# A convolution and channel-mix kernel: its start written out in a fixed order, with a first step of 256 tokens, small first groups and a new order of loads

## The chip, the cores and the metric

The kernel runs on one core of one Trainium2 chip. The time is device microseconds (us) of that core. A core has TensorE (PE; PEld is its weight load), VectorE (DVE), ScalarE (ACT), GpSimd (POOL) and SyncE (SP). They run side by side and wait for one another through semaphores. SBUF is the working memory, PSUM the memory that TensorE writes. DMAs are issued here from two queues: SP's and POOL's.

## What is computed

The input `x` is 8 batches x 4160 tokens x 192 channels. A causal convolution over 7 tokens, with softmax weights per head (8 heads of 24 channels), is followed by a channel mix:

```python
# convolution: w = softmax(weight, axis=-1); 8 heads x 7 taps
out = np.einsum('hk,bskhg->bshg', w, x_unf)            # x_unf: the 7 tokens up to s
# channel mix, on x = out
x_prev = np.concatenate([zeros, x[:, :-1, :]], axis=1)
xk = mu_k * x + (1.0 - mu_k) * x_prev
xr = mu_r * x + (1.0 - mu_r) * x_prev
k = np.maximum(xk @ w_k, 0.0)                          # 192 -> 1024
v = k * k @ w_v                                        # 1024 -> 192
r = 1.0 / (1.0 + np.exp(-(xr @ w_r)))                  # 192 -> 192
return r * v
```

## The kernel before

**Tiling.** Batches are worked on in four pairs `p`. Of a pair, both batches go through the same instructions. The convolution works in blocks of 112 tokens (38 blocks cover 4160 tokens), and several blocks make a group: 9 or 10, for the first pair 5, 5, 10, 9 and 9. For a group, POOL loads x as bf16 with the halo of 6 tokens (`load_x`, lines 71-95). `conv_mm` (193-205) multiplies a head's 24 channels of all blocks by a banded (Toeplitz) matrix `toe`, one matmul and one PSUM bank a head. `conv_out` (207-219) copies the result to `y`, whose channels are kept as 128 of batch one, 128 of batch two, and the last 64 of both together. Then tokens and channels are exchanged: for the early groups on TensorE (`tr_mm` 246-258, up to six transposes of two blocks, and `tr_out` 260-268 on DVE), for all others by writing `y` to DRAM and reading it back through a transposing DMA (`y_write` 229-236, `y_read` 238-243, both on SP).

**Channel mix.** Steps have 512 tokens of both batches, the last of a pair 64. `diff` (275-286) and four `mix` (288-321) make `xk` and `xr` on DVE. Each step has eight slots, one for 128 of the 1024 hidden channels: `k_mm` (329-355) on TensorE, `k_relu` (378-384) on ACT, `k_square` (386-396) on DVE. The output side goes in tiles of 128 tokens: `r_mm` and `r_sig` (400-421), `v_mm` with eight matmuls (423-437), `v_out` (439-456) with the store on SP.

**Order.** All engines work through their instructions in the order in which the code gives them. Four tables (`early`, `pe`, `act`, `dve`) hold what is done in which slot `n`, and slots are worked off in pairs (516-530): first the early loads, then the k matmuls of both slots, then for each slot ACT's copies, TensorE's other matmuls, the relu, DVE's work and the square of the slot before. A v tile is worked on ten slots after the k slot of the same number (`LAG_V`). Slots run from -60, so the same tables also give the start: group 0 is convolved from slot -22 on, with ACT and DVE taking turns at its copies, group 1 from slot -7 on, step 0 is mixed from slot -7 to -2. A matmul that needs a PSUM buffer waits for the copy that empties it; the convolution, the transposes and r share two buffers (`psM`), k has two (`psK`) and v two (`psV`).

**The start (lines 98-187).** SP loads the convolution weights and the six pieces of `mu`. 36 matmuls on constants (122-126) keep TensorE busy; they read `ones_t` and the zeroed `w_row`. DVE and ACT compute the softmax into `w_row` (127-144), SP writes it to DRAM (`w_scr`) and reads it back, shifted per partition, as `toe` (146-155). POOL loads x of group 0 at once; then a copy from `w_row` (186) holds its queue until the softmax is there; then follow `wk`, x of group 1, `wr`, `wv` and further x. POOL's DMAs take turns at eight semaphores, so a DMA waits until the one eight places before it has landed. The three buffers of `xb` also hold loads back until an older group is convolved.

Lines of helpers that appear in the profile: L88 is the large x load, L124 the warm-up, L139 the last step of the softmax, L199 the convolution, L216 and L219 its copies, L254 and L265 transposes and their copies, L281 `diff`, L303 `mix`, L343 and L350 the two halves of k, L382 relu, L396 square, L412 and L413 r, L421 sigmoid, L431 v, L443 output.

Of the kernel before, what the change touches and what calls it, by code (L numbers as in the profile page):

```python
# [7 lines left out]
FP32 = mybir.dt.float32  # L8
# [6 lines left out]
def kernel(  # L15
# [23 lines left out]
    NBLK = -(-S // BLK)  # L39
    STEP = 512  # L40
    NSTEP = S // STEP
    TAIL = S - NSTEP * STEP
    NPAIR = B // 2
    SPP = NSTEP * NF + 1
    NSLOT = NPAIR * SPP
    YC = 16
    LAG_V = NF + 2
    WARM = 36
    LAG_R = NF
# [11 lines left out]
    groups = [  # L61
        [(0, 10, 0), (10, 10, 2), (20, 9, 4), (29, 9, 6)]
        if p
        else [(0, 5, 0), (5, 5, 1), (10, 10, 2), (20, 9, 4), (29, 9, 6)]
        for p in range(NPAIR)
    ]
# [4 lines left out]
    def load_x(p, g):  # L71
        blk0, nb, _ = groups[p][g]
        xb = three.tile([P, GB, 2, D], BF16, tag="xb", name="xb")
        xbs[p, g] = xb
        for s in range(2):
            b = 2 * p + s
            lo, hi = 0, nb
            if blk0 == 0:
                lo = 1
                nc.gpsimd.memset(xb[0:32, 0, s, :], 0.0)  # L80
                nc.gpsimd.dma_start(out=xb[HALO:P, 0, s, :], in_=x[b, 0 : P - HALO, :])
            t0 = blk0 * BLK - HALO
            if blk0 + nb == NBLK:
                hi = nb - 1
                r0 = t0 + hi * BLK
                nc.gpsimd.memset(xb[:, hi, s, :], 0.0)
                nc.gpsimd.dma_start(out=xb[0 : S - r0, hi, s, :], in_=x[b, r0:S, :])
# [11 lines left out]
    nc.sync.dma_start(  # L99
        out=w_raw,  # L100
        in_=bass.AP(tensor=weight.tensor, offset=weight.offset, ap=[[0, P], [K, H], [1, K]]),
    )
    nc.scalar.preload_act_table(AF.Exp)
    ones_t = const.tile([P, P], BF16)
    nc.vector.memset(ones_t, 1.0)
# [3 lines left out]
    nc.vector.memset(w_row, 0.0)  # L109
    load_x(0, 0)  # L110
    ident = const.tile([P, P], BF16)
    nc.gpsimd.affine_select(
        out=ident,
        in_=ones_t,
        pattern=[[1, P]],
        compare_op=ALU.is_equal,
        fill=0.0,
        base=0,
        channel_multiplier=-1,
    )  # L120

    warm = psM.tile([P, 4, P], FP32, tag="m", name="warm")
    for _ in range(WARM):
        nc.tensor.matmul(  # L124
            out=warm, lhsT=ones_t, rhs=w_row[:, 0:4, :], start=True, stop=True
        )
    w_max = const.tile([P, H], FP32)
    nc.vector.tensor_reduce(out=w_max, in_=w_raw, axis=mybir.AxisListType.X, op=ALU.max)
    w_exp = const.tile([P, H, K], FP32)
    nc.vector.tensor_tensor(  # L130
        out=w_exp, in0=w_raw, in1=w_max.unsqueeze(2).to_broadcast([P, H, K]), op=ALU.subtract
    )
    nc.scalar.activation(out=w_exp, in_=w_exp, func=AF.Exp)
    w_sig = const.tile([P, 1], FP32)
    nc.scalar.activation(out=w_sig, in_=w_exp[:, 0, 0:1], func=AF.Sigmoid)
    w_sum = const.tile([P, H], FP32)
    nc.vector.tensor_reduce(out=w_sum, in_=w_exp, axis=mybir.AxisListType.X, op=ALU.add)
    nc.vector.reciprocal(out=w_sum, in_=w_sum)
    nc.vector.tensor_tensor(  # L139
        out=w_row[:, :, 0:K],  # L140
        in0=w_exp[:, :, ::-1],
        in1=w_sum.unsqueeze(2).to_broadcast([P, H, K]),
        op=ALU.mult,
    )
    w_scr = dram.tile([P, H, P], BF16)
    nc.sync.dma_start(out=w_scr, in_=w_row)
    toe = const.tile([P, H, BLK], BF16)
    nc.sync.dma_start(
        out=toe,
        in_=bass.AP(  # L150
            tensor=w_scr.tensor,
            offset=w_scr.offset + K - 1,
            ap=[[H * P - 1, P], [P, H], [1, BLK]],
        ),
    )


    mu = const.tile([P, 2, 2], FP32)
    for i, m in enumerate((moe_mu_k, moe_mu_r)):
        nc.sync.dma_start(out=mu[:, i, 0:1], in_=m[0:P])  # L160
        nc.sync.dma_start(out=mu[0:LO, i, 1:2], in_=m[P:D])
        nc.sync.dma_start(out=mu[LO:P, i, 1:2], in_=m[P:D])
# [8 lines left out]
    def load_w(w, src):  # L171
        nc.gpsimd.dma_start(out=w[:, 0, :], in_=src[0:P, :])
        nc.gpsimd.dma_start(out=w[0:LO, 1, :], in_=src[P:D, :])
        nc.gpsimd.dma_start(out=w[LO:P, 1, :], in_=src[P:D, :])

    def load_rest():
        load_w(wr, moe_w_r)
        nc.gpsimd.memset(wr[:, 2:4, :], 0.0)
        nc.gpsimd.tensor_copy(out=wr[0:LO, 2, :], in_=wr[0:LO, 1, :])
        nc.gpsimd.tensor_copy(out=wr[LO:P, 3, :], in_=wr[LO:P, 1, :])  # L180
        nc.gpsimd.dma_start(out=wv, in_=moe_w_v.rearrange("(f p) d -> p f d", p=P))
        for t in tails:
            nc.gpsimd.memset(t, 0.0)

    gate = const.tile([P, 1], BF16)
    nc.gpsimd.tensor_copy(out=gate, in_=w_row[:, 0, 0:1])
    load_w(wk, moe_w_k)


    ys, yTs = {}, {}  # L190
    conv_ps = {}

    def conv_mm(p, g, h):
        nb = groups[p][g][1]
        if h == 0:
            ys[p, g] = two.tile([P, GB, 2 * D], BF16, tag="y", name="y")
        ps = psM.tile([P, GB, 2, G], FP32, tag="m", name="ps_c")
        conv_ps[p, g, h] = ps
        nc.tensor.matmul(  # L199
            out=ps[:BLK, :nb],  # L200
            lhsT=toe[:, h, :],
            rhs=xbs[p, g][:, :nb, :, h * G : (h + 1) * G],
            start=True,
            stop=True,
        )
# [355 lines left out]
```

## Time and profile before

| | |
|---|---|
| time, median of three runs | 486.33 us (485.29 to 487.19) |
| the profiled execution | 485.83 us, of it span from first to last instruction 484.1 us |
| mean granted TensorE clock | 0.979 |
| busy: PE, DVE, ACT, POOL | 459.3, 390.5, 374.6, 51.9 us |
| PE without any idle time | from 54.6 to 470 us |
| first convolution matmul, first relu | 20.94 us, 31.03 us |

The profile is one execution. Times are from the span's start. A releaser named behind `<-` is what ended an idle time. The granted clock is the share of full speed that TensorE's throttle gave in a stretch.

### The profile page before, as it was taken

The page shows a single profiled execution, that of the slowest core. Times are in us where ns is not written, and L with a number is a line of the kernel's source. Part 1 is how long each engine was busy: PE and PEld are TensorE (multiplying, and loading weights), DVE is VectorE, ACT ScalarE, POOL GpSimd, SP SyncE. Part 2 cuts the span into 40 slices and gives each one's busy share as a digit, 9 for nine tenths or more (in the row PEclk, how much of TensorE's full clock was granted, in tenths as well). Part 3 has the DMA queues.
Part 4 walks back from the last instruction along what each step waited for, and adds up shares of the span by engine and source line. Part 5 has one row for each costly group of instructions (what it writes and reads, how often), then busy time and mean ns, then how long its engine had stood idle before and what let it go on. Part 6 is the DMA issues. An engine that isn't in the chain of part 4 may idle for free.

```text
span 484.1 us, 9846 instructions
## 1 busy us (share of the span) xinstructions
PE 459.3 (95%) x3920; PEld 299.0 (62%) x3920; DVE 390.5 (81%) x607; ACT 374.6 (77%) x544; POOL 51.9 (11%) x84
## 2 busy tenths in 40 slices
PE   8167799999999999999999999999999999999996
PEld 3133466666667666666667666666667666666676
DVE  1165698989889887988889887988889887999873
ACT  2137879798887889798887889798887879777772
POOL 3560401002030101002030101002000000000000
PEclk9668999999999999999999999999999999999999
DMA  3898696938959492948759392947935351712112
GB/s 43 133 154 100 96 188 140 208 110 157 167 125 216 83 249 67 186 132 154 172 119 217 78 233 86 190 134 144 180 121 139 108 144 53 190 67 67 67 57 99
DMA packets 137837, 65.03 MB, mean 134 GB/s; under 512 B 89344, under 2 KB 137408, under 8 KB 137792
## 3 DMA queue, kind: packets, MB, share of 16 engines
q1 hardware_dynamic: 97200, 48.80, 41.8%
q0 software_dynamic: 40592, 15.62, 28.0%
q8 instruction: 30, 0.49, 0.5%
q14 instruction: 15, 0.12, 0.1%
HBM read 31.49 MB, written 37.18 MB: 142 GB/s over the span
## 4 chain that ended last, share of the span: by engine, by line
PE 90%; DMA 4%; ACT 2%; POOL 2%; DVE 1%; issue 0%; DVEq 0%; POOLq 0%
PE ps_v L431 35%; PE ps_k L343 25%; PE ps_k L350 14%; PE ps_c L199 4%; PE ps_r L413 4%; PE ps_r L412 4%; DMA xb<-in_x_dram 3%; PE warm L124 2%; DMA wr<-in_moe_w_r_dram 1%; POOL xb L88 1%; ACT k_sb L382 1%; ACT y L216 1%; ACT y L219 0%; PE ps_t L254 0%; PE ps_k L370 0%; PE ps_k L363 0%
## 5 line engine op out<-in xcount | busy, mean ns | idle before, releaser
L382 ACT ACTIVATE k_sb<-ps_k 128x1024 bf16<-128x1024 f32 x260 | 259.9, 1027 | 34.3 <-PE ps_k L350 30.8
L431 PE MATMUL ps_v<-wv,k 128*128 128x192 bf16 x2048 | 210.8, 246 | 0.0
L431 PEld LDWEIGHTS <-k 128*128 128x128 bf16 x2048 | 175.2, 98 | 30.3
L396 DVE TENSOR_TENSOR k<-k_sb 128x1024 bf16<-128x1024 bf16 x256 | 175.0, 684 | 20.2 <-ACT k_sb L382 19.6
L343 PE MATMUL ps_k<-xk,wk 128*128 128x512 bf16 x512 | 155.2, 385 | 0.0
L443 DVE TENSOR_TENSOR o_sb<-ps_v,r_sb 128x384 f32<-128x384 f32 x132 | 72.3, 547 | 36.7 <-PE ps_v L431 35.4
L421 ACT ACTIVATE r_sb<-ps_r 128x384 bf16<-128x384 f32 x132 | 64.2, 486 | 40.8 <-PE ps_r L413 40.8
L350 PE MATMUL ps_k<-xk,wk 64*128 64x512 bf16 x512 | 78.7, 385 | 0.0
L343 PEld LDWEIGHTS <-wk 128*128 128x128 bf16 x512 | 37.7, 97 | 54.5 <-issue 53.9
L216 ACT CAST y<-ps_c 112x480 bf16<-112x480 f32 (+5 forms) x99 | 47.8, 489 | 23.8 <-PE ps_c L199 19.7
L303 DVE SCALAR_TENSOR_TENSOR xk<-d,mu,yT 128x1024 bf16<-128x1024 bf16 x64 | 64.7, 1013 | 0.1
L303 DVE SCALAR_TENSOR_TENSOR xr<-d,mu,yT 128x1024 bf16<-128x1024 bf16 x64 | 64.5, 1012 | 0.1
L199 PE MATMUL ps_c<-xb,toe 128*112 128x432 bf16 (+2 forms) x136 | 47.6, 359 | 17.3 <-DMA toe<-w_scr 9.1
L412 PE MATMUL ps_r<-wr,xr 128*128 128x192 bf16 x256 | 63.0, 246 | 1.0 <-ACT y L219 1.0
L413 PE MATMUL ps_r<-wr,xr 128*128 128x192 bf16 x256 | 63.0, 246 | 0.0
L350 PEld LDWEIGHTS <-wk 64*128 64x128 bf16 x512 | 15.9, 94 | 56.1 <-issue 55.6
L88 POOL DMA_DIRECT2D xb<-in_x_dram x34 | 32.4, 957 | 119.7 <-PE ps_c L199 69.0
L199 PEld LDWEIGHTS <-toe 128*112 128x112 bf16 x136 | 18.4, 136 | 26.5 <-DMA toe<-w_scr 9.6
L281 DVE TENSOR_TENSOR d<-yT 128x1536 bf16<-128x1536 bf16 (+1 forms) x36 | 31.6, 877 | 0.1
L219 ACT CAST y<-ps_c 112x432 bf16<-112x432 f32 (+5 forms) x49 | 24.7, 511 | 1.7 <-PE ps_c L199 1.6
L413 PEld LDWEIGHTS <-xr 128*128 128x128 bf16 x256 | 25.0, 98 | 1.3 <-issue 1.2
L412 PEld LDWEIGHTS <-xr 128*128 128x128 bf16 x256 | 25.0, 98 | 0.8 <-issue 0.7
(52 smaller groups left out, 91.0 us busy)
## 6 DMA issues: line engine op xcount, KB each, us to landing
out_dram<-o_sb SPq DMA_DIRECT2D x128, 192.0 KB, 2.2
xb<-in_x_dram POOLq DMA_DIRECT2D x14, 432.0 KB, 11.8
y_dram<-y SPq DMA_DIRECT2D x8, 756.0 KB, 7.0
y_dram<-y SPq DMA_DIRECT2D x6, 840.0 KB, 5.5
xb<-in_x_dram POOLq DMA_DIRECT2D x8, 480.0 KB, 11.1
xb<-in_x_dram POOLq DMA_DIRECT2D x8, 384.0 KB, 9.6
xb<-in_x_dram POOLq DMA_DIRECT2D x2, 240.0 KB, 7.1
xb<-in_x_dram POOLq DMA_DIRECT2D x2, 192.0 KB, 4.4
```

Of the source, the lines that this page charges most:

```text
L199: nc.tensor.matmul(out=ps[:BLK, :nb], lhsT=toe[:, h, :], rhs=xbs[p, g][:, :nb, :, h * G : (h + 1) * G], start=True, stop=True,)
L216: copy(out=yh[:, :, :, c0 : c0 + n], in_=ps[:BLK, :nb, :, 0:n])
L303: nc.vector.scalar_tensor_tensor(out=o, in0=d[r0:r1, sl, :L], scalar=mu[r0:r1, i, part : part + 1], in1=yT[r0:r1, sl, c0 : c0 + L], op0=AL ...
L343: nc.tensor.matmul(out=ps[:, i, :], lhsT=wk[:, 0, fs], rhs=xk[:, i, :], start=first, stop=not first)
L350: nc.tensor.matmul(out=ps[:, i, :], lhsT=wk[r, 1, fs], rhs=xk[r, 2, :], start=not first, stop=first)
L382: nc.scalar.activation(out=k_sb, in_=ps.rearrange("p a b -> p (a b)"), func=AF.Relu)
L396: nc.vector.tensor_tensor(out=o, in0=k_sb, in1=k_sb, op=ALU.mult)
L412: nc.tensor.matmul(out=o, lhsT=hi, rhs=wr[:, 0, :], start=True, stop=False)
L413: nc.tensor.matmul(out=o, lhsT=lo, rhs=wlo, start=False, stop=True)
L421: nc.scalar.activation(out=r_sb[:, :n, :], in_=ps[:, :n, :], func=AF.Sigmoid)
L431: nc.tensor.matmul(out=o, lhsT=k2[:, f, t * P : (t + 1) * P], rhs=wv[:, f, :], start=(f == 0), stop=(f == NF - 1),)
L443: nc.vector.tensor_tensor(out=o_sb[:, :n, :], in0=v_ps.pop(m)[:, :n, :], in1=r_sbs.pop(m)[:, :n, :], op=ALU.mult)
```

## The change

The work ahead of the first slot no longer comes out of the slot tables: `prologue()` writes it out in one fixed order, and slots begin at 0. In it:

- The first pair has steps of 256, seven of 512, 256 and 64 tokens instead of eight of 512 and one of 64. A step of 256 has four slots, each with two times 128 hidden channels, so that a slot has the same number of columns.
- The groups of the first pair have 3, 4, 5, 4, 10, 6 and 6 blocks. The first four are transposed on TensorE, the last three through DRAM. Small groups put up to three heads into one PSUM bank (`chunks`), with one copy for all of them; in the prologue the convolution uses `psM` and `psV` in turn.
- The warm-up has 34 matmuls and reads an own tile `zeros`.
- Memsets of the x halo and of `wr` go from POOL to DVE. The two copies inside `wr` become two more loads of the same rows.
- `toe` is read on POOL's queue; behind it follow `wk`, x of group 2, `wr`, `wv`, x of group 3. The copy that held POOL back is gone. SP loads `mu` after writing `w_scr`.
- The slots of the first groups' work are set anew (`late`, `per`).

```diff
-    WARM = 36
+    WARM = 34
...
+    for p in range(NPAIR):
+        sizes = [STEP // 2] + [STEP] * (S // STEP - 1) + [STEP // 2] if p == 0 else [STEP] * (S // STEP)
...
+        for nb, s, on_pe in (
+            ((3, 0, True), (4, 1, True), (5, 2, True), (4, 3, True), (10, 4, False), (6, 6, False), (6, 7, False))
+            if p == 0
+            else ((10, 0, False), (10, 2, False), (9, 4, False), (9, 6, False))
+        ):
...
+    def chunks(g):
+        n = max(1, min(3, BANK // (2 * G * groups[g][2])))
+        return [range(h, min(H, h + n)) for h in range(0, H, n)]
...
+        def go(hi, start):
+            for f in range(nf):
+                fs = slice((j * nf + f) * P, (j * nf + f + 1) * P)
+                for i in range(2):
+                    r = slice(0, P) if hi else slice(i * LO, (i + 1) * LO)
+                    nc.tensor.matmul(
+                        out=ps[:, i, f * L : (f + 1) * L],
...
+            at_ = n0 + ns + 2
+            tiles.append((s, t, max(at_, tiles[-1][2] + 1) if tiles else at_))
...
+        late = p == 0 and n0 < 30
+        if not on_pe:
+            per = 2 if late else 1
+            c0 = n0 - 20 if late else n0 - 30
+            w0, r0 = c0 + -(-nc_ // per), n0 - (11 if late else 17)
+        else:
+            per = 1
+            c0 = n0 - 14 if n0 > 12 else 1
+            r0 = c0 + nc_ + 1
...
+    def prologue():
...
+        nc.vector.memset(ones_t, 1.0)
+        nc.vector.memset(zeros, 0.0)
+        x_tile(0, nc.vector)
+        x_tile(1, nc.vector)
+        x_tile(2, nc.vector)
+        nc.vector.memset(w_row, 0.0)
+        nc.vector.memset(wr[:, 2:4, :], 0.0)
+        load_x(0)
+        load_x(1)
...
+        warm = psK.tile([P, BANK], FP32, tag="k", name="warm")
+        for _ in range(WARM):
+            nc.tensor.matmul(out=warm, lhsT=ones_t, rhs=zeros, start=True, stop=True)
+        softmax()
+        nc.sync.dma_start(out=w_scr, in_=w_row)
+        load_toe()
+        load_wk()
+        load_x(2)
+        load_wr()
+        load_wv()
...
+        for c in range(n):
+            conv_mm(0, c, psV if c % 2 else None, "v" if c % 2 else "m")
+        for c in range(n):
+            conv_out(0, c, act_ if c % 2 == 0 else dve_, act_)
+        for j in range(2):
+            tr_mm(0, j)
+        for j in range(2):
+            tr_out(0, j, dve_)
+        n = len(chunks(1))
+        for c in range(n):
+            conv_mm(1, c, psV if c % 2 else None, "v" if c % 2 else "m")
+            conv_out(1, c, act_)
+        diff(0)
+        for i in range(2):
+            for part in range(2):
+                mix(0, i, part)
+        for j in range(2):
+            tr_mm(1, j)
+            tr_out(1, j, dve_)
+        x_tile(3, nc.vector)
+        load_x(3)
```

Three places show how rows move. On POOL's queue, from the making of the identity matrix on, there stood before (a name in brackets is a semaphore; `DMASW` are those of POOL's own DMAs, `DMAHW` those of SP's):

```order
L112 AFFINE_SELECT ident<-ones_t 128x128 [waits DVE_49]
L186 COPY gate<-w_row 128x1 [waits DVE_49]
L172 DMA wk<-in_moe_w_k_dram 128x1024
L173 DMA wk<-in_moe_w_k_dram 64x1024
L174 DMA wk<-in_moe_w_k_dram 64x1024
L88 DMA xb<-in_x_dram 128x5x192
L88 DMA xb<-in_x_dram 128x5x192 [waits DMASW0_49]
L172 DMA wr<-in_moe_w_r_dram 128x192 [waits DMASW1_49]
```

and there stands now, at the same place:

```order
L527 AFFINE_SELECT ident<-ones_t 128x128
L174 DMA toe<-w_scr 128x8x112 [waits DMAHW1_49]
L142 DMA wk<-in_moe_w_k_dram 128x1024
L143 DMA wk<-in_moe_w_k_dram 64x1024 [waits DMASW0_49]
L144 DMA wk<-in_moe_w_k_dram 64x1024 [waits DMASW1_49]
L109 DMA xb<-in_x_dram 128x5x192 [waits DMASW2_49]
L109 DMA xb<-in_x_dram 128x5x192 [waits DMASW3_49]
L147 DMA wr<-in_moe_w_r_dram 128x192 [waits DMASW4_49]
```

The copy that waited for the softmax is gone, the toe load with its wait for `w_scr` stands ahead of all weights, and the x load in this row is that of group 2, since group 1 went out before.

On DVE, from the last step of the softmax to the first step's mix, there stood before:

```order
L139 TENSOR_TENSOR w_row<-w_exp,w_sum 128x8x7 [waits DVE_49,PE_49]
L216 CAST y<-ps_c 112x5x2x24 [waits PE_49] x2
L216 CAST y<-ps_c 112x5x2x8 [waits PE_49]
L219 CAST y<-ps_c 112x5x2x16
L219 CAST y<-ps_c 112x5x2x24 [waits PE_49]
L226 MEMSET yT 128x3x8
L265 COPY yT<-ps_t 128x3x224 [waits PE_49] x2
L265 COPY yT<-ps_t 128x3x112 [waits PE_49]
L281 TENSOR_TENSOR d<-yT 128x1536 [waits DVE_49]
L303 SCALAR_TENSOR_TENSOR xk<-d,mu,yT 128x1024 [waits DMAHW1_49,DVE_49]
```

and there stands now:

```order
L166 TENSOR_TENSOR w_row<-w_exp,w_sum 128x8x7 [waits DVE_49]
L219 CAST y<-ps_c 112x3x2x56 [waits PE_49]
L227 MEMSET yT 128x3x8
L268 COPY yT<-ps_t 128x3x224 [waits PE_49]
L268 COPY yT<-ps_t 128x3x112 [waits PE_49]
L281 TENSOR_TENSOR d<-yT 128x3x256 [waits DVE_49]
L301 SCALAR_TENSOR_TENSOR xk<-d,mu,yT 128x2x256 [waits DMAHW2_49,DVE_49]
```

The softmax's last step no longer waits for PE, one copy of group 0 is left on DVE, and difference and mix are half as long.

On ACT, from the first relu on, there stood before (copies of groups of 10 and 9 blocks between the relus):

```order
L382 ACTIVATE k_sb<-ps_k 128x1024 [waits PE_49]
L219 CAST y<-ps_c 112x5x2x24 [waits PE_49]
L382 ACTIVATE k_sb<-ps_k 128x1024
L216 CAST y<-ps_c 112x10x2x24 [waits DVE_49,PE_49,Activation_49]
L382 ACTIVATE k_sb<-ps_k 128x1024 [waits PE_49]
L216 CAST y<-ps_c 112x10x2x24 [waits PE_49]
L216 CAST y<-ps_c 112x9x2x24 [waits PE_49,Activation_49]
L382 ACTIVATE k_sb<-ps_k 128x1024
```

and there stands now:

```order
L372 ACTIVATE k_sb<-ps_k 128x1024 [waits PE_49] x2
L219 CAST y<-ps_c 112x5x2x48 [waits PE_49,Activation_49]
L372 ACTIVATE k_sb<-ps_k 128x1024 [waits PE_49]
L219 CAST y<-ps_c 112x5x2x48 [waits PE_49]
L372 ACTIVATE k_sb<-ps_k 128x1024
L219 CAST y<-ps_c 112x5x2x32 [waits PE_49]
L222 CAST y<-ps_c 112x5x2x16
L372 ACTIVATE k_sb<-ps_k 128x1024 [waits DVE_49,PE_49]
```

Between the first relus stand copies of group 2, two heads each; those of the group of ten blocks come from slot 9 on.

More of the change, by code (lines that the diff above doesn't have):

```diff
@@ L108 @@
     w_row = const.tile([P, H, P], BF16)
[L109 to L136, printed above, removed]
@@ L185 @@
[L185 to L190, printed above, removed]
-    conv_ps = {}
[L193 to L205, printed above, removed]
@@ L357, in k_mm_tail @@
-    def k_mm_tail(n):
-        p, s, f = where(n)
+        s, j = slots[n]
+        p, _, L, _, _ = steps[s]
+        if L == TAIL:
+            return k_mm_tail(n, p)
+        xk = xks[s]
+        ps = psK.tile([P, 2, BANK], FP32, tag="k", name="ps_k")
+        k_ps[n] = ps
+        first = j % 2 == 0
+        nf = STEP // L
+        def go(hi, start):
[3 more added lines that the diff above has]
+                    r = slice(0, P) if hi else slice(i * LO, (i + 1) * LO)
+                    nc.tensor.matmul(
+                        out=ps[:, i, f * L : (f + 1) * L],
+                        lhsT=wk[r, 0 if hi else 1, fs],
+                        rhs=xk[r, i if hi else 2, :L],
+                        start=start and f == 0,
+                        stop=not start and f == nf - 1,
+                    )
@@ L518, with bundles @@
+    def bundles():
+        n = 0
+        while n < tiles[-1][2] + 3:
+            w = 2 if n < NSLOT and steps[slots[n][0]][2] > TAIL else 1
+            yield range(n, n + w)
+            n += w
+    with tc.manual_schedule():
+        prologue()
+        for n in range(-60, 0):
+            for table in (early, act, pe, dve):
+                assert n not in table, n
+        for ns in bundles():
             for n in ns:
                 run(early, n)
-            real = [n for n in ns if 0 <= n < NSLOT]
+            real = [n for n in ns if n < NSLOT]
```

433 lines of the change are left out of this document (226 added, 207 removed).

## The prediction

> **What bounds the kernel now.** I read the profile's stages first (busy time of each engine between two moments of the span), because the page's shares mix a start-up with a steady state. Columns: stretch, length, then busy time of PE, PEld, DVE, ACT and POOL with instruction counts, granted clock, DMA share, GB/s.
>
> ```profile
> 0.00:12.00 12.00, 10.17 (x36) 4.08 (x36) 1.62 (x7) 3.02 (x4) 3.71 (x11) 1.00 0.40 43
> 12.00:21.00 9.00, 0.06 (x1) 0.06 (x2) 0.09 (x1) 0.00 (x0) 5.65 (x10) 0.75 1.05 162
> 21.00:30.00 9.00, 7.04 (x32) 4.01 (x32) 5.91 (x13) 3.82 (x12) 6.37 (x9) 0.50 0.88 91
> 30.00:42.00 12.00, 7.85 (x35) 2.81 (x34) 5.07 (x9) 4.66 (x7) 3.42 (x6) 0.71 1.59 190
> 42.00:54.60 12.60, 8.77 (x47) 3.81 (x47) 9.59 (x14) 12.11 (x22) 2.29 (x5) 1.00 0.12 14
> 54.60:470.00 415.40, 415.40 (x3651) 274.39 (x3649) 363.32 (x559) 347.16 (x493) 30.46 (x44) 1.00 0.71 141
> ```
>
> From 54.6 to 470 us TensorE is never idle at full clock: there only TensorE work counts, and the change adds or removes hardly any. All that can be won lies before 54.6: warm-up matmuls on constants, 9 us of nothing, 21 us at half or mixed clock, and 12.6 us in which ACT is the full engine (12.11 of 12.60). The chain that ended last and the list of waits name the causes.
>
> ```profile
> 1.67 10.18 PE warm L124 x36
> 28.12 12.99 DMA xb<-in_x_dram
> ```
>
> ```profile
> DVE w_row L139 <- PE warm L124: 6.0, 1, 6.0
> PE ps_c L199 <- DMA toe<-w_scr: 9.1, 1, 9.1
> PE ps_c L199 <- DMA xb<-in_x_dram: 3.6, 2, 3.0
> ```
>
> The softmax result is kept back 6.0 us by the warm-up (which reads `w_row`), TensorE then waits 9.1 us for `toe`, and later 3.6 us for x of the third and fourth group. The timeline gives the moments:
>
> ```profile
> 5.64 0.20 DVE L138 RECIPROCAL w_sum<-w_sum 128x8 f32<-128x8 f32 x1
> 11.87 0.22 DVE L139 TENSOR_TENSOR w_row<-w_exp,w_sum 128x56 bf16<-128x56 f32 x1 [6.03 <-PE warm L124]
> 20.94 0.65 PE L199 MATMUL ps_c<-xb,toe 128*112 128x240 bf16 x2 [9.11 <-DMA toe<-w_scr]
> 31.03 1.02 ACT L382 ACTIVATE k_sb<-ps_k 128x1024 bf16<-128x1024 f32 x1 [1.04 <-PE ps_k L350]
> ```
>
> **The measure.** Since the end is TensorE without a gap, the time is decided by TensorE's debt when that stretch begins: the moment minus the useful TensorE work done by then, at full-clock prices. The prices are in the chain behind 54.6 (start, length, what):
>
> ```profile
> 54.80 0.43 PE ps_k L343 x2
> 55.23 0.54 PE ps_k L350 x4
> 55.77 0.54 PE ps_k L343 x2
> 56.31 0.30 PE ps_t L254 x6
> 56.61 0.66 PE ps_v L431 x8
> 57.27 0.08 PE ps_r L412
> 70.13 0.18 PE ps_c L199
> ```
>
> The first three rows are two k slots: 1.51, so 0.755 a slot. A v tile is 0.66, an r tile 2 x 0.08 = 0.16, six transposes 0.30 (0.15 a block of 112 tokens), a convolution matmul of nine blocks 0.18 (0.02 a block and head, 0.16 a block). Before, at 54.6, ten slots (7.55), the convolution of 5+5+10+9 = 29 blocks (4.64), transposes of ten blocks and six more (1.8) and one r tile (0.16) are done: 14.2. **Debt before: 54.6 - 14.2 = 40.4 us.**
>
> **The change part by part.** *Softmax and toe.* The warm-up now reads `zeros`, so `w_row` loses its wait for PE and starts where the reciprocal ends: 5.84 + 0.22, about 6.1 instead of 12.1. The memsets that DVE gets now (zeros, x halo, wr) stand ahead of the softmax, where DVE only waits for the weights to land; that wait covers them, and beyond it they would delay `w_row` one for one. The transfers, with KB each and median us from issue to landing; the row under them is the shortest, median and longest landing of the large x loads, and the last is what POOL pays to issue one (mean ns):
>
> ```profile
> w_scr<-w_row SPq DMA_DIRECT2D x1, 256.0 KB, 2.0
> toe<-w_scr SPq DMA_DIRECT2D x1, 224.0 KB, 6.7
> xb<-in_x_dram POOLq DMA_DIRECT2D x2, 192.0 KB, 4.4
> xb<-in_x_dram POOLq DMA_DIRECT2D x2, 240.0 KB, 7.1
> wk<-in_moe_w_k_dram POOLq DMA_DIRECT2D x1, 256.0 KB, 4.8
> y_dram<-y SPq DMA_DIRECT2D x8, 756.0 KB, 7.0
> yT<-y_dram SPq DMA_TRANSPOSE x14, 8.9
> DMA to landing us min/median/max: 4.4/10.1/17.9
> L88 POOL DMA_DIRECT2D xb<-in_x_dram x14 | 13.2, 949 | 0.3 <-issue 0.3
> ```
>
> `w_scr` goes out at 6.1 and lands 2.0 later; with first x loads beside it I take toe's issue at 8.4. On POOL the toe load is ahead of wk, x and wr, and what is queued behind its wait is exactly those. Toe itself: not below 4.4 (192 KB with nothing beside it), not above 6.7 (what it took beside wk and x); I take 5.0, nearer the first, since only the end of two x loads is ahead of it. **Toe at T = 13.4** (12.8 to 15.1) instead of 20.9. The mu loads now follow `w_scr` on SP; they are first read about T + 4, so they have some 7 us.
>
> The page "DMA: Bandwidth & Descriptors" of the Trainium skill (Specifications) gives a first-byte latency of about 1 us on the GpSimd path and 0.6 on the SyncE path, which speaks against moving toe to POOL; by it the sum would be 0.4 us longer, an estimate that no run here shows.
>
> *From toe to the first relu.* Before it took 31.03 - 20.94 = 10.1 us, with five blocks a group, 512 tokens and half clock. The prices on ACT and DVE (busy, mean ns):
>
> ```profile
> L382 ACT ACTIVATE k_sb<-ps_k 128x1024 bf16<-128x1024 f32 x13 | 13.9, 1078 | 2.0 <-PE ps_k L350 2.0
> L216 ACT CAST y<-ps_c 112x480 bf16<-112x480 f32 x5 | 2.9, 578 | 4.4 <-issue 3.2 <-PE ps_c L199 1.3
> L216 ACT CAST y<-ps_c 112x240 bf16<-112x240 f32 x8 | 2.7, 358 | 18.8 <-PE ps_c L199 18.5
> L421 ACT ACTIVATE r_sb<-ps_r 128x384 bf16<-128x384 f32 x2 | 1.0, 492 | 1.1 <-PE ps_r L413 1.1
> L265 DVE COPY yT<-ps_t 128x672 bf16<-128x672 bf16 x7 | 3.5, 507 | 9.6 <-PE ps_t L254 9.5
> L281 DVE TENSOR_TENSOR d<-yT 128x1536 bf16<-128x1536 bf16 x3 | 2.9, 958 | 0.1
> ```
>
> Between the two copy rows a copy of other size is read off a straight line (432 elements 0.53, 384 0.49, 288 0.40). Group 0: matmuls and their latency 0.45, ACT's copies with one wait for DVE 1.55, so T + 2.0; nine transposes 0.5; two DVE copies 0.5 + 0.35, T + 3.4. Only then are its PSUM buffers free for group 1, whose five ACT copies take 2.1: T + 5.6; its transposes stand on PE ahead of the first k matmul: T + 6.6; one slot and its latency 1.0: **first relu at T + 7.6 = 21.0**, 10 us earlier than before. DVE's half-size difference and mixes (0.5 + 0.5 + 0.4 after T + 3.4) hide under group 1, as does wk (issued by 12.3, landing 4.8 later, 17.1). Bounds 7 to 10.1 for the stretch.
>
> *The first fourteen slots.* v tiles of whole steps now begin at slot 14. ACT has to do, slots 0 to 13: 14 relus x 1.08 = 15.1; copies of group 2 (three of 480, and 320 + 160) 2.4; of group 3 (three of 384, and 256 + 128) 2.1; of group 4 (seven of 480, and 320 + 160) 4.8; two sigmoids 1.0. Sum 25.4; before, ACT was busy 12.11 of 12.60 in such a stretch, 96%, so 26.4. The k matmuls of slot 14 start about a relu before relu 14: T + 7.6 + 26.4 - 1.0 = **46.4**. TensorE's work by then: 14 slots 10.6; convolution of 3+4+5+4+10 = 26 blocks 4.2; transposes of 16 blocks 2.4; four v tiles 2.6; six r tiles 1.0: 20.8. **Debt after: 46.4 - 20.8 = 25.6.** The stretch can be 2 us shorter (no bubble, relus at 1.0) or 4 longer, since four matmuls in a row now pass two PSUM buffers.
>
> *Loads behind toe.* At 0.95 an issue: wk to 12.2, x of group 2 to 14.1, landing 7.1 after its issue, 20.3; the x load of group 3 waits for that landing, group 4's two follow, the last issued at 22.2. At the median 10.1 it lands at 32.3. Its first matmul is in slot 8: eight relus, group 2, one copy of group 3 and the sigmoids are 12.5 / 0.96 = 13 us after T + 7.6, less one for TensorE's lead: 33. In time by 0.7 us; cost 0, and 7 if it takes the longest landing, 17.9.
>
> *Steady part and end.* The rest of the order is the same rows, in other group sizes for the first pair; ACT has spare time there (347 of 415). Half-size matmuls are more in number, but columns are equal: 0, at most 0.5. The transposed read of group 4 is asked for in slot 17 and needed by DVE in slot 21; DVE will wait. Write out at 45.4, 7.0, then 8.9: 61.3. TensorE can go on to slot 24's v tile: 46.4 + 10 x 1.70 (0.755 + 0.66 + 0.16 + six blocks 0.12) = 63.4, less the difference, square and output that DVE owes first, 2.2: 61.2. Cover just holds: 0.
>
> **Sum.** The profiled execution took 485.8 (span 484.1, 1.7 around it), 0.5 under the median of the three runs, 486.3. Debt falls by 40.4 - 25.6 = 14.8: 485.8 - 14.8 = **471.0**.
>
> **Rivals.** *A: as summed.* For it: every stretch has its price in a row. 0.52, with 467 to 474 from the bounds above (toe -0.6 to +1.7, first relu to +2.5, ACT -2 to +4, not all at once).
>
> *B: the x stream is late.* For it: before, the longest piece of the chain is an x load (12.99), and the load of group 4 has 0.7 us to spare by the median. Against: fewer bytes are ahead of it, and TensorE waits for x only twice in all (3.6 us). At 17.9 it lands at 40.1, TensorE and ACT stand 7.1 in slot 8: 478; half of it, 474.5. 0.22.
>
> *C: the clock falls in the sparse prologue.* The clock in the third column from the end:
>
> ```profile
> 16.00:18.00 2.00, 0.00 (x0) 0.00 (x0) 0.00 (x0) 0.00 (x0) 1.81 (x4) 0.62 1.11 198
> 32.00:34.00 2.00, 1.32 (x8) 0.61 (x6) 1.07 (x2) 1.33 (x3) 1.06 (x3) 0.62 1.60 191
> ```
>
> A mean of 0.62 over 2 us is a quarter at full and the rest at half: it fell near 16.5, 4.6 us after the last warm-up matmul (1.67 + 10.18 = 11.85), and came back near 33.5, 12.6 us after TensorE resumed. Now the warm-up of 34 ends near 11.3, and toe is 2.1 us behind: not long enough by that row. But from T to T + 6.6 TensorE has about 2.5 us of work, and the clock may fall there. Then for up to 12.6 us a slot costs TensorE some 1.3 x 2 = 2.6 us against ACT's 26.4 / 14 = 1.9: 0.7 over nearly five slots, 3.4, and about 1 in the prologue: 475.4. 0.18. The page "TensorE: Matmul & The Clock Gate" of the Trainium skill (Part 1) has the clock back after one busy window of about 3.4 us; by it this rival would cost about 1 us and 1 in the prologue, 473. The trace speaks against so short a time here: PE was busy 2 of 2 us at half clock between 30 and 32 and 7.04 of 9 before, and the clock stayed down.
>
> *D: the transposed read of group 4 stops DVE.* Its place is the difference in slot 21, asked for four slots earlier instead of ten. With the read landed at 61.2 it costs nothing; each us later costs one, since TensorE then waits for PSUM that DVE must empty. If both the write and the read take as long as the longest x load (17.9), it lands at 45.4 + 35.8 = 81.2: 20 us, 491, slower than before; it decides from 76 on. Against: the medians are 7.0 and 8.9, and the x loads beside it are smaller. 0.03.
>
> *E: less waiting than summed* (toe near 12.8, ACT without bubbles): 464 to 467. 0.05.
>
> **How the numbers follow.** The likeliest is A, 471.0. The range takes A, most of B and C: 465 to 478; outside are D, the low half of E and the worst of B and of several delays together, under 2 in 10. A measurement of this kernel can tell about 0.5% (2.4 us) from no change: 483.9 to 488.7. A, B, C and E are faster than that, 0.97, of which I keep 0.02 for delays that add up to no change: faster 0.95, same 0.02, slower 0.03.
>
> **What would show it.** In the profile after: `w_row` without a wait for PE, near 6; the first convolution near 13.4; the first relu near 21; TensorE without idle time from about 46 on; the wait for x in slot 8 under 1 us; granted clock 1.0 from 12 on (C: 0.5 somewhere in 14 to 30). Wrong would be: toe later than 15, ACT under 90% between 22 and 46, a DVE wait for `yT` that TensorE feels, or a gap-free stretch that begins after 50.

## The result, and the profile after

The changed kernel takes **469.03 us** (468.94 to 469.93, four runs); the kernel before took 486.76 beside it (485.29 to 488.14). The ratio is 0.964, with a 95% interval of 0.961 to 0.967. Forecast: 471.0, within 465 to 478. The profiled execution took 468.94, its span is 467.2 instead of 484.1: 16.9 us less.

The stages after: stretch, length, busy time of PE, PEld, DVE, ACT and POOL with counts, granted clock, DMA share, GB/s.

```profile
0.00:12.00 12.00, 8.94 (x34) 3.67 (x34) 2.39 (x10) 3.02 (x4) 7.07 (x15) 1.00 0.72 92
14.00:21.00 7.00, 5.55 (x41) 3.95 (x41) 5.71 (x12) 2.46 (x9) 6.85 (x12) 0.54 1.36 163
21.00:44.70 23.70, 19.86 (x157) 11.51 (x157) 19.14 (x30) 21.20 (x35) 5.62 (x8) 0.99 1.04 129
46.00:452.00 406.00, 397.81 (x3514) 269.67 (x3572) 356.11 (x554) 341.49 (x494) 29.58 (x36) 1.00 0.70 144
```

The 9 us without work are gone, half clock fills only the prologue, and the first fourteen slots lie from 21 to 45. The 8 us that TensorE lacks in the last row aren't idle time: 3514 matmuls are recorded beside 3572 weight loads. From 46 us to the end the list of TensorE's waits has this one entry:

```profile
PE ps_k L343 <- issue: 0.2, 1, 0.2
```

The chain, first piece by piece to the first convolution, then through DVE ahead of slot 14, and into the gap-free stretch (start, length, what):

```profile
0.80 2.88 DMA w_raw<-in_weight_dram
...
4.96 0.23 DVE w_row L166
...
5.21 4.21 DMA w_scr<-w_row
...
9.71 3.44 DMA toe<-w_scr
...
38.79 0.56 DVE o_sb L446
39.35 0.60 DVE k L391
39.95 1.20 DVE xr L301
41.15 0.60 DVE k L391
41.75 0.43 DVE yT L268
...
42.22 0.36 PE ps_c L199
...
44.72 1.58 PE ps_k L343 x8
...
46.42 0.66 PE ps_v L433 x8
```

`w_row` is ready at 5.2, nine tenths of a microsecond earlier than forecast (the weights land 2.88 after their issue, with no `mu` loads beside them now); `w_scr` takes twice what it took before; toe, with 3.44 instead of 5.0, makes up for it. The v tile of slot 14 starts at 46.42, its k matmuls at 44.72. The timeline beside it:

```profile
13.19 0.71 PE L199 MATMUL ps_c<-xb,toe 128*112 128x144 bf16 x8 [2.86 <-DMA toe<-w_scr]
20.90 2.06 ACT L372 ACTIVATE k_sb<-ps_k 128x1024 bf16<-128x1024 f32 x2 [2.61 <-PE ps_k L343]
46.26 0.82 PE L433 MATMUL ps_v<-wv,k 128*128 128x192 bf16 x8
```

First convolution 13.19 (forecast 13.4), first relu 20.90 (21.0). The timeline merges the v tile with a convolution matmul ahead of it, hence 46.26; this row is what the runs below are compared by. TensorE has no wait for x in its list, and DVE waits 0.2 us for the transposed read:

```profile
PE ps_c L199 <- DMA toe<-w_scr: 2.9, 1, 2.9
DVE d L281 <- DMA yT<-y_dram: 0.2, 1, 0.2
```

### The profile page after: what moved, and what is told of

It is laid out like the page before. It is cut to its first block, busy times and chain, and to the rows that moved or that the text cites. A ratio compares the mean times of both kernels' runs of the same rounds, so it can differ in the third digit from the quotient of the medians.

```text
span 467.2 us, 9868 instructions
## 1 busy us (share of the span) xinstructions
PE 445.2 (95%) x3892; PEld 300.6 (64%) x3954; DVE 390.4 (84%) x616; ACT 374.6 (80%) x549; POOL 51.1 (11%) x71
## 4 chain that ended last, share of the span: by engine, by line
PE 91%; ACT 2%; issue 2%; DMA 2%; DVE 1%; DVEq 0%; ACTq 0%
PE ps_k L343 38%; PE ps_v L433 37%; PE ps_c L199 5%; PE ps_r L416 5%; PE ps_r L415 5%; ACT k_sb L372 1%; DMA w_scr<-w_row 1%; PE ps_k L360 1%; DMA toe<-w_scr 1%; ACT y L219 1%; DMA w_raw<-in_weight_dram 1%; PE ps_t L257 1%; DVE yT L268 0%; ACT y L222 0%; DVE k L391 0%
## 5 line engine op out<-in xcount | busy, mean ns | idle before, releaser
L343 PE MATMUL ps_k<-xk,wk 64*128 64x512 bf16 (+2 forms) x994 | 206.0, 376 | 9.5 <-ACT k_sb L372 0.9
L343 PEld LDWEIGHTS <-wk 64*128 64x128 bf16 (+1 forms) x1056 | 56.2, 96 | 109.2 <-issue 107.9
L301 DVE SCALAR_TENSOR_TENSOR xr<-d,mu,yT 128x1024 bf16<-128x1024 bf16 (+1 forms) x66 | 65.1, 988 | 0.1
L301 DVE SCALAR_TENSOR_TENSOR xk<-d,mu,yT 128x1024 bf16<-128x1024 bf16 (+1 forms) x66 | 64.4, 977 | 0.2
L219 ACT CAST y<-ps_c 112x480 bf16<-112x480 f32 (+4 forms) x100 | 47.9, 483 | 10.4 <-PE ps_c L199 10.2
L199 PE MATMUL ps_c<-xb,toe 128*112 128x480 bf16 (+5 forms) x152 | 46.2, 332 | 5.3 <-DMA toe<-w_scr 2.9
L109 POOL DMA_DIRECT2D xb<-in_x_dram x38 | 34.9, 928 | 26.8 <-PE ps_c L199 15.9
L281 DVE TENSOR_TENSOR d<-yT 128x1536 bf16<-128x1536 bf16 (+2 forms) x37 | 31.8, 859 | 0.4 <-DMA yT<-y_dram 0.2
L108 POOL DMA_DIRECT2D xb<-in_x_dram x8 | 4.3, 538 | 215.7 <-PE ps_k L343 206.3
L222 ACT CAST y<-ps_c 112x480 bf16<-112x480 f32 (+8 forms) x53 | 25.2, 482 | 0.2 <-DVE yT L227 0.2
L103 POOL DMA_DIRECT2D xb<-in_x_dram x8 | 4.6, 581 | 62.4 <-PE ps_r L416 61.0
```

Of the source, the lines that this page charges most:

```text
L109: nc.gpsimd.dma_start(out=xb[:, lo:hi, s, :], in_=bass.AP(tensor=x.tensor, offset=x.offset + (b * S + t0 + lo * BLK) * D, ap=[[D, P], [BLK ...
L199: nc.tensor.matmul(out=ps[:BLK, :, :, i * G : (i + 1) * G], lhsT=toe[:, h, :], rhs=xbs[g][:, :nb, :, h * G : (h + 1) * G], start=True, sto ...
L219: copy(out=yh[:, :, :, c0 : c0 + n], in_=ps[:BLK, :, :, 0:n])
L301: nc.vector.scalar_tensor_tensor(out=o, in0=d[r0:r1, sl, :L], scalar=mu[r0:r1, i, part : part + 1], in1=yT[r0:r1, sl, c0 : c0 + L], op0=AL ...
L343: nc.tensor.matmul(out=ps[:, i, f * L : (f + 1) * L], lhsT=wk[r, 0 if hi else 1, fs], rhs=xk[r, i if hi else 2, :L], start=start and f == ...
```

## Experiments

All runs compute the whole result; each was timed beside the kernel before (medians 486.05 to 486.86). "v tile" is the timeline's start of slot 14's first v tile, "half clock" the stretch at a granted clock of 0.50 that holds the prologue, both, like the first convolution and the span, from the profiled execution, while the time is a median.

| run | time | interval of the ratio | first convolution | half clock | v tile | span |
|---|---|---|---|---|---|---|
| changed kernel | 469.03 | 0.961-0.967 | 13.19 | 14.58-21.40 | 46.26 | 467.2 |
| warm-up with zeros in the kernel before | 478.58 | 0.982-0.989 | 17.07 | 16.08-29.73 | | 477.0 |
| warm-up on `w_row` | 474.06 | 0.973-0.977 | 18.10 | 16.18-26.42 | 51.47 | 472.4 |
| toe on SP | 475.54 | 0.976-0.980 | 18.88 | 16.81-30.46 | 53.37 | 474.3 |
| one head a bank | 471.43 | 0.967-0.972 | 13.65 | 13.90-24.14 | 49.13 | 470.1 |
| warm-up of 47 | 468.61 | 0.962-0.968 | 13.17 | 18.25-21.66 | 46.03 | 467.0 |
| x of group 1 behind toe | 467.68 | 0.961-0.966 | 11.88 | 15.75-22.58 | 45.72 | 466.7 |
| steps of 512 | 480.18 | 0.986-0.992 | 13.36 | 15.30-25.54 | | 478.4 |
| clock kept up | 468.18 | 0.961-0.966 | 13.98 | none | 45.45 | 466.4 |
| read 3 slots later | 472.67 | 0.970-0.975 | 13.19 | 17.38-20.79 | 45.83 | 470.7 |
| x behind toe, clock kept up | 467.20 | 0.959-0.963 | 12.09 | none | 44.73 | 465.7 |
| xr mix later | 469.94 | 0.964-0.969 | 14.11 | 15.04-25.28 | 48.55 | 470.9 |
| all three | 468.08 | 0.959-0.964 | 11.86 | none | 44.57 | 466.2 |

**The warm-up's wait**, taken out of the kernel before, and put back into the changed one:

```diff
 # kernel before
+    zeros = const.tile([P, 4, P], BF16)
+    nc.vector.memset(zeros, 0.0)
-            out=warm, lhsT=ones_t, rhs=w_row[:, 0:4, :], start=True, stop=True
+            out=warm, lhsT=ones_t, rhs=zeros, start=True, stop=True
 # changed kernel
-            nc.tensor.matmul(out=warm, lhsT=ones_t, rhs=zeros, start=True, stop=True)
+            nc.tensor.matmul(out=warm, lhsT=ones_t, rhs=w_row[:, 0:4, :], start=True, stop=True)
```

> The kernel before with one edit: the warm-up reads a tile of zeros of its own, so the softmax result no longer waits for it. Theory (TensorE's debt at the start of its gap-free stretch decides, and toe's moment moves it one for one): the softmax result stands near 6 instead of 12.1, toe lands near 15 instead of 20.9, the loads behind POOL's waiting copy start 6 us earlier too, so the whole start moves by 6: 480.8. Rival (the start is bound by how fast its loads come, not by when they are asked for): the x of the third and fourth group lands at most 3 earlier: 483.8 or more. If the first is right, some 11 of the 17 us of the change come from other parts.

> The changed kernel with the warm-up reading w_row again, as before. Theory: the softmax result waits for the warm-up's end (10.3 in the changed kernel) plus 0.2, 10.6 instead of 5.2; the write of w_scr then has no x load beside it and takes 2.0 as before instead of 4.2, so toe lands 3.2 later: 472.2. Rival, loads: wk and x of group 2 are queued behind toe and come later too, and x of group 4, which had a microsecond or two to spare, holds up slot 8: 475. Rival, no effect (the start has slack for toe): 469.0.

478.58: the two lines alone bring the kernel before 7.7 us, more than either theory gave them. The first convolution and the first relu (27.16) came only 3.9 earlier; behind them TensorE waited 2.4 us for x instead of 3.6, and the clock, back at 29.73, did not fall again as it did in the kernel before from 36.94 to 40.35. 474.06: put back into the changed kernel, the wait costs 5.0 us, for a first convolution 4.9 later, one for one. It is not the full 6 us of the wait, because `w_scr` then goes out beside nothing and takes half as long. Its DMA rows (KB, median us to landing), and then those of the changed kernel:

```profile
w_scr<-w_row SPq DMA_DIRECT2D x1, 256.0 KB, 2.0
toe<-w_scr POOLq DMA_DIRECT2D x1, 224.0 KB, 4.2
```

```profile
w_scr<-w_row SPq DMA_DIRECT2D x1, 256.0 KB, 4.2
toe<-w_scr POOLq DMA_DIRECT2D x1, 224.0 KB, 3.4
```

**Toe's queue.** One line of the load of toe:

```diff
-        nc.gpsimd.dma_start(
+        nc.sync.dma_start(
```

> The changed kernel with one edit: toe is read on SP's queue, as before, so that POOL's wk, x and wr are no longer behind it. Theory (what counts is that toe is ahead of the weights): POOL issues wk and x from about 6.5 on, toe shares the engines with them and takes the 6.7 it took before, from about 9.6: 16.3 instead of 13.2, so 472.1. Rival (the queue does not matter, the engines are shared in any case): toe lands within 0.5 of 13.2, the weights land 4 earlier, time 468.5 to 469.5.

475.54: 6.5 us slower, beyond what either theory said. Its DMA row and that of the load of `wk` beside it:

```profile
toe<-w_scr SPq DMA_DIRECT2D x1, 224.0 KB, 8.9
wk<-in_moe_w_k_dram POOLq DMA_DIRECT2D x1, 256.0 KB, 7.0
```

On POOL's queue the toe load stands ahead of the weights, and its wait holds them back; on SP's, POOL issues `wk` and x at once, and toe lands 8.9 after its issue instead of 3.4. Two things change with the queue: this order, and the pieces (packets) in which the load moves. The packets in the traces are 64 of up to 4256 bytes on POOL's queue and 1024 of 224 bytes on SP's. Their own times, divided by the 16 DMA engines, come to 0.9 and 1.75 us; between the first and the last of them other packets, almost all from POOL's queue, took 0.2 and 5.0 us. So the smaller packets account for about 1 us of the 5.5, an estimate from these sums, and sharing with POOL's loads for most of the rest; no run here held those loads back with toe on SP. The first convolution came 5.7 later. The v tile came 7.1 later, and the clock stayed at half until 30.46, past the first relu at 26.97, which fits the difference.

**Several heads a bank.**

```diff
-        n = max(1, min(3, BANK // (2 * G * groups[g][2])))
+        n = 1
...
-            per = 1
+            per = 2
...
-            r0 = c0 + nc_ + 1
+            r0 = c0 + nc_ // 2 + 1
```

> The changed kernel with one head to a PSUM bank everywhere (two matmuls and copies a slot for the groups that are transposed on TensorE, so that their slots stay as they are). Theory (ACT is the full engine up to slot 14): a copy has a fixed part of 0.14 (240 elements 0.358, 480 elements 0.578); groups 2 and 3 have eight more copies in slots 1 to 10, 1.1, and group 1 four more in the prologue, 0.6, group 0 some 0.3: 471.0, with ACT busier between 21 and 46. Rival (ACT was busy only 21.2 of 23.7 us there, copies fit into its idle time): 469.0 to 469.5.

471.43: 2.4 slower, on the theory's side. The v tile came 2.9 later, 0.5 of it already there at the first convolution (`w_scr` took 4.6). How much of the rest is the copies and how much the clock, which stayed down until 24.14 here, the run doesn't tell.

**The clock.** A longer warm-up, and then matmuls on constants in the prologue's gaps as well (47, and 2, 2 and 3 behind the first convolution, the first transposes and the second convolution):

```diff
-    WARM = 34
+    WARM = 47
...
+        keep(2)
...
+        keep(2)
...
+        keep(3)
```

> The changed kernel with 47 warm-up matmuls instead of 34: 13 more at 0.216 end near 13.1, where toe lands, so TensorE is not idle for the 2.9 us between 10.3 and 13.2. Theory (the clock at 0.5 between 14.6 and 21.4 is due to that gap and lengthens the chain from toe to the first relu): the clock stays at 1.0, the transposes, convolutions and first k matmuls on the chain (0.57 + 0.49 + 1.11 + 1.41 at half clock) shrink by some 1.6: 467.4. Rival 1 (the clock falls all the same, since TensorE's work after toe is sparse): 469.0. Rival 2 (the chain is ACT's and DVE's copies, the clock does not matter): clock 1.0 and 469.0.

> The changed kernel with 47 warm-up matmuls and seven more of them in TensorE's idle times behind toe: two behind the convolution of group 0, two behind its transposes, three behind the convolution of group 1. With 47 alone the clock held to 18.2, fell to 0.5 until 21.3, the first relu came 0.6 earlier. Theory (the half clock behind toe is due to sparse work and costs what TensorE's pieces of the chain lose, 1.4 in all of which 0.6 are won already): clock 1.0 all through, first relu near 19.6 instead of 20.9, time 467.7. Rival 1 (the added matmuls stand in the chain's way and take back what the clock gives): first relu 20.3 or later, 468.6 or more. Rival 2 (the first relu moves, but the stretch behind it is bound by ACT and takes it back): 469.0.

468.61 and 468.18. Both lie within 0.5% of 469.03, so the profile has to say it: with one window of half clock left, the v tile comes 0.23 earlier, and with the clock at 1.00 throughout 0.81, against a median 0.85 lower. But these 0.8 are net of what the added matmuls cost, as rival 1 had it: the 47 lasted until 14.14 there, so the first convolution began at 13.98, 0.79 later, and from it to the v tile the way is 1.6 shorter (31.47 instead of 33.07). Half clock costs 0.8 to 1.6 here.

**The x load in front of toe.** `load_x(1)` moves behind `load_toe()`:

```diff
         load_x(0)
-        load_x(1)
...
         load_toe()
+        load_x(1)
```

> The changed kernel with the x load of group 1 issued behind toe instead of ahead of it. Theory (the write of w_scr took 4.2 instead of 2.0 because the x loads of group 1 ran beside it): w_scr lands near 7.5, toe near 10.9, 2.2 earlier; time down by up to 2.2: 466.8, if x of group 1 (issued from 8.4 to 10.3, landing 5.1 later, 15.4) does not hold up its convolution, which comes 2.9 after toe, 13.8; with that wait of 1.6 the gain is 0.6: 468.4. Rival (w_scr was slow for another reason, the mu loads beside it): w_scr lands near 9.4 still, toe near 13, x of group 1 and the weights come 2 later: 469 to 471.

> Both edits that look like gains together: x of group 1 behind toe (toe at 11.9, 467.7), 41 warm-up matmuls (they end where toe lands) and the seven fillers behind toe. Theory (toe's moment and the clock behind it add): first relu near 18.3, time 466.4. Rival (with toe earlier, x of group 1 and the weights are late next, so the clock gives nothing more): first relu near 19.5, 467.7.

The DMA rows of the first of these:

```profile
w_scr<-w_row SPq DMA_DIRECT2D x1, 256.0 KB, 2.3
toe<-w_scr POOLq DMA_DIRECT2D x1, 224.0 KB, 4.0
```

`w_scr` is back at 2.3, so the x load of group 1 was what made it 4.2. The convolution starts 1.3 earlier and the first relu 1.4, but the v tile only 0.54, and the time falls 1.35 to 467.68. The clock was at half until 22.58 here, 1.2 later than in the changed kernel, and the third relu, at 22.71, was only 0.59 earlier. With the clock kept up as well (41 matmuls in the warm-up) it is 467.20 us, 0.961 of the kernel before (0.959 to 0.963); its five runs (466.94 to 467.40) all lie below the four of the changed kernel. The first relu came at 18.73, between theory and rival, and the rival's reason shows: TensorE waits 1.1 us for x of group 2, which the changed kernel doesn't.

**Steps of 512.** The first pair again with eight steps of 512 and one of 64, and its groups' work in other slots:

```diff
-        sizes = [STEP // 2] + [STEP] * (S // STEP - 1) + [STEP // 2] if p == 0 else [STEP] * (S // STEP)
+        sizes = [STEP] * (S // STEP)
...
+        if p == 0:
+            n0 = {2: 8, 3: 20, 4: 28, 5: 44, 6: 52}[g]
```

> The changed kernel with all steps of 512 tokens (the groups and their slots as in the changed kernel; both first groups are transposed before the first difference). Theory (the small first step counts because it lets k begin before group 1 is through): difference and both k mixes of 512 tokens (0.96 + 1.28 + 0.75) now stand behind the copies of group 1's transposes on the chain to the first relu, +2.9, and the second step, now due in slot 8, is ready only after the transposes of group 2, another 1 to 2: 473 to 474. Rival (TensorE has to convolve and transpose the same blocks before the gap-free stretch, and ACT has the same copies to do, so step size does not matter): 469.0 to 469.5.

480.18, far beyond both. The first relu came 3.0 later, as expected; much of the rest is a new wait of TensorE, for the mixes of the second step:

```profile
PE ps_k L343 <- DVE xk L301: 5.0, 3, 2.8
```

Behind it the clock fell twice more (35.78 to 39.19 and 42.61 to 49.43). The slots had to be laid out anew for this, so the run prices that layout and not the size of the step alone; that price stays open.

**The transposed read's cover.** The read of group 4 is asked for three slots later:

```diff
-            w0, r0 = c0 + -(-nc_ // per), n0 - (11 if late else 17)
+            w0, r0 = c0 + -(-nc_ // per), n0 - (8 if late else 17)
```

> The changed kernel with the transposed read of group 4 asked for in slot 20 instead of 17; DVE needs it in slot 21. It landed at 56.3 with DVE waiting 0.2 us; three slots later it should land near 61.3 and DVE wait some 5. Theory (TensorE goes on until PSUM that DVE owes it runs out, at slot 24's v tile: 44.7 + 10 x 1.7 = 61.7, less 2.2 of DVE work): 59.5, so 1.8 of the wait are felt: 470.8. Rival 1 (DVE is needed at once, the wait counts in full): 474. Rival 2 (the read is hidden deeper than that, for k of that step begins only in slot 28): 469.0.

Its waits between 50 and 72 us (engine, line, releaser: us in total, times, longest):

```profile
DVE d L281 <- DMA yT<-y_dram: 7.4, 1, 7.4
...
ACT k_sb L372 <- DVE k L391: 2.7, 1, 2.7
PE ps_v L433 <- DVE o_sb L446: 2.1, 1, 2.1
```

472.67, between the expected numbers. The v tile of slot 14 is 0.43 earlier than in the changed kernel and the span 3.5 longer, so a wait of 7.4 cost 3.9: TensorE went on until 63.0, then stood 2.1, and then ran at half clock for 3.4 us (65.2 to 68.6), which is another 1.7.

**The mix ahead of the copies.** In the changed kernel's chain DVE's xr mix (1.20) stands ahead of the yT copy. Moved behind it, in the changed kernel and in the fastest:

```diff
-            at(dve, n0 + ((-3, -2, -1, 0)[j] if late else j - 5), mix, s, i, part)
+            at(dve, n0 + ((-3, -2, 2, 3)[j] if late else j - 5), mix, s, i, part)
```

> The changed kernel with one edit: the two xr mixes of the steps of 256 (VectorE, 1.20 us) stand three slots later in the order, behind group 3's first copies of yT instead of ahead of them. Theory: in the changed kernel the chain of waits runs through VectorE in slots 8 to 12 (xr from 39.95 to 41.15 us, then k, then the yT copy that ps_c waits for), so the mix's 1.2 us come off the path: the v tile of slot 14 starts near 45.2 us in place of 46.42, and the time is 467.6 to 467.9 us. Rival: ScalarE, busy for 21.20 of the 23.7 us from 21.0 to 44.7 and for all 4.0 us from 42 to 46, is the bound there and takes it back: the v tile of slot 14 stays within 0.3 us of 46.4, and the time is 469.0 us.

> The kernel with the x load behind the toe matrix and the clock kept up (467.20 us), with the xr mixes three slots later as well. Theory: the mix is on the path here too, and the v tile of slot 14 starts near 43.7 us in place of 44.90: 465.9 to 466.3 us. Rival, ScalarE takes it back: 467.2 us. Below 466.0 us would say that the three gains add in full.

469.94 and 468.08: nothing won. In the first, whose profiled execution took 472.65, 2.7 above its median, `w_scr` took 4.8 and the clock came back at 25.28, so its v tile tells nothing; in the second, whose clock kept up, the v tile came 0.16 earlier. Its chain shows why:

```profile
37.92 1.02 ACT k_sb L372
38.95 0.50 ACT y L219
...
39.48 0.47 PE ps_t L257 x6
...
39.98 0.52 DVE yT L268
```

The mix is gone from it, and a relu and a copy on ACT stand there instead. The theory of the mix falls: ACT, busy throughout from 42 to 46 in the changed kernel and in these two, and DVE are late together, and where DVE is relieved, ACT ends last. The mix is missed later: behind slot 14 TensorE waits for DVE's output, 1.2 us in the first and 0.4 in the second, where the changed kernel has no such wait.

## Why the prediction was right, and where it was not

**The measure held.** Debt when the gap-free stretch begins: 44.72 - 20.8 = 23.9, against 40.4 before: the rule makes that 16.5 us, and the span fell by 16.9. In the runs a shift of the v tile is a shift of the span almost one for one: +5.21 and +5.2 (warm-up on `w_row`), +7.11 and +7.1 (toe on SP), +2.87 and +2.9 (one head a bank), -0.54 and -0.5, -0.81 and -0.8, -1.53 and -1.5. The exceptions have a stop of TensorE behind slot 14, for DVE's output: read later (2.1 us), xr mix later (1.2) and all three (0.4; v tile -1.69, span -1.0).

**Softmax and toe.** The wait of the warm-up goes, as said. The forecast of 13.4 came out at 13.19 by errors that cancel: `w_row` 0.9 early, `w_scr` 4.2 instead of the 2.0 to 2.3 that were taken, toe 3.44 instead of 5.0. The row from which `w_scr` was priced came from a moment with nothing beside it; the x loads in front were the cause, which moving one of them showed.

**The price of the toe queue.** The page "DMA: Bandwidth & Descriptors" of the Trainium skill (Specifications) has the shorter first-byte latency on SP's path; in this case SP's was the slower by 5.5 us (8.9 and 3.4), most of it for the loads that POOL issues meanwhile. Place in the order outweighed the path, whose latency no run here shows by itself.

**Toe to first relu** was priced at 7.6 and took 20.90 - 13.19 = 7.7, half clock included. That is luck: with the clock kept up it took 6.2 (20.22 - 13.98) and, in the fastest run, 6.6 (18.73 - 12.09), so the price was 1.0 to 1.4 too long for full clock, and half clock, which sum A did not have, filled it.

**The fourteen slots** are the mis-sized term: 26.4 forecast from first relu, less one; k of slot 14 came at 44.72 instead of 46.4. The step that failed is "Sum 25.4; before, ACT was busy 12.11 of 12.60 in such a stretch, 96%". ACT was busy 21.20 of 23.70, 89%, and still finished 1.7 earlier, because listed durations overlap when instructions stand back to back:

```profile
L372 ACT ACTIVATE k_sb<-ps_k 128x1024 bf16<-128x1024 f32 x14 | 14.6, 1047 | 3.8 <-PE ps_k L343 3.7
```

A relu is listed with 1.05 there, but two in a row take 1.94, as the timeline of the same run shows:

```profile
43.38 1.94 ACT L372 ACTIVATE k_sb<-ps_k 128x1024 bf16<-128x1024 f32 x2
```

The stretch holds the 35 instructions of the sum, and their listed durations (counts times means) add up to 25.1, beside 21.2 of busy time. So the sum of 25.4 was too long by about 4, while the idle time that was taken as 4% is 11%: two errors that partly cancel, by luck, and leave 1.7. The profile before already had the hint, for in its stretch of 12.60 the 22 listed durations add up to 16.6 beside 12.11 of busy time.

**x of group 4** was in time, at cost 0; rival B did not happen. Its last load was issued at 21.18 and took 10.0 to land, and its first matmul started at 34.92, so some 3 us were to spare instead of 0.7. **The transposed read** cost nothing, as forecast, but came 5 us earlier than summed: the write went out at 43.44 instead of 45.4 and took 5.4 instead of 7.0, the read, asked for at 50.56, took 5.7 instead of 8.9, and it landed at 56.3 instead of 61.3. The rule of rival D (each us past 61.2 costs one) gives 1.8 for the read that landed at 62.97. TensorE stood 2.1 for it, so the rule was near, though by terms that cancel: slot 14 came 2 us earlier than it took, but a v tile stands 1.7 behind its k matmuls (44.72 and 46.42). What it left out is the clock, which fell after that stop and cost most of the other 1.8.

**Rival C** did happen: the clock fell at 14.58. But it cost 0.8 to 1.6, not 4.4, since it was back before the second relu. Why, the rows say: stretch, and behind the length PE's busy time, then, third from the end, the clock. First the kernel before, then the changed one:

```profile
26.70:30.11 3.41, 2.85 (x9) 1.22 (x8) 3.34 (x6) 2.39 (x8) 2.44 (x3) 0.50 1.39 150
30.11:33.53 3.42, 3.15 (x14) 1.09 (x13) 2.48 (x3) 1.94 (x3) 0.59 (x2) 0.50 1.59 188
33.53:36.94 3.41, 0.43 (x3) 0.24 (x3) 1.11 (x2) 0.37 (x1) 2.82 (x5) 1.00 1.60 191
```

```profile
11.16:14.58 3.42, 0.87 (x10) 0.68 (x10) 0.54 (x2) 0.74 (x3) 3.42 (x7) 1.00 1.00 177
14.58:17.99 3.41, 2.56 (x19) 2.01 (x17) 2.38 (x6) 1.69 (x7) 3.38 (x7) 0.50 1.35 169
17.99:21.40 3.41, 3.23 (x25) 1.93 (x24) 3.34 (x7) 0.80 (x2) 3.30 (x6) 0.50 1.40 153
21.40:24.82 3.42, 3.22 (x27) 2.04 (x26) 3.42 (x5) 3.40 (x6) 0.75 (x1) 1.00 1.30 136
```

The stretches at half clock last 3.41, 6.83, 10.24, 13.65 or 17.07 us in these runs: one to five times 3.41. The clock is decided by windows of that length, and it came back at the end of the first window in which TensorE was busy nearly throughout (3.15 and 3.23 of 3.41 here; 2.85 was not enough). The page "TensorE: Matmul & The Clock Gate" of the Trainium skill (Part 1) says just that: free-running windows of 3413 ns, full clock after one busy window. The prediction held the trace against that page of the Trainium skill ("PE was busy 2 of 2 us at half clock between 30 and 32"); that reading was wrong, since those 2 us lie, but for 0.1, inside one window, and at its end, 33.53, the clock came back. The 12.6 us were not the clock's delay but three windows that weren't full enough. By that page of the Trainium skill the rival would have cost 2, nearer to what was measured.

## What to carry to other kernels

Where the end is an engine without a gap, price a change by that engine's debt at the moment from which it runs through; shifts of that moment then read off as time, one for one. For a chain of DMAs ahead of everything, count the loads that run beside each link and put the others behind it: that was worth 6.5 us for the toe load (the smaller packets included) and 1.35 for x of group 1. Sum an engine's work from its pace in a busy stretch, not from listed durations, and judge the clock by whole windows.

## What the hardware showed

- The phase of the clock's windows differs between executions, and with it the luck of a sparse start. The changed kernel and the one with the later read are the same up to slot 14, and both start the convolution at 13.19, yet half clock held two windows in the one and one in the other, and the v tile differs by 0.43 us. With a warm-up of 47 the mean clock was 1.000 in two executions (468.53 and 467.85) and 0.994 and 0.995 in two others (468.76 and 468.70). The windows of the later read:

```profile
17.38:20.79 3.41, 3.14 (x24) 1.94 (x24) 3.36 (x7) 0.81 (x4) 3.39 (x6) 0.50 1.46 166
20.79:24.21 3.42, 3.36 (x30) 2.15 (x28) 3.40 (x5) 3.42 (x5) 1.23 (x2) 1.00 1.38 153
```

- A busy share does not settle it alone: a window with 3.16 of 3.41 was not enough with one head a bank, while 2.95 was in the kernel before with zeros and 2.88 with steps of 512. The records miss some matmuls, so the bound can't be read more closely.
- The write of 256 KB to DRAM took 2.0 to 2.6 us with at most the x loads of one group beside it and 4.1 to 4.8 with those of two.
- The same load of 224 KB moved in 64 packets of up to 4256 bytes from POOL's queue and in 1024 packets of 224 bytes from SP's; their times add up to 0.9 and 1.75 us of the 16 engines.
